# A grouped-query decode kernel on one core: the last step of V turned, output summed in PSUM, head epilogues on ScalarE

## The chip, the cores and the metric

The kernel runs on one core of a Trainium2 chip. The metric is device time in microseconds (us) of one execution; a profile's span is about 2 us shorter than the timed execution, because it runs from the first instruction to the last. Engines are named as in the profile: PE is TensorE (PEld its weight loads), DVE is VectorE, ACT is ScalarE, POOL is GpSimd, SP is SyncE, whose queue issues the large loads (SPq). "Granted clock" is the share of the full TensorE clock that the throttle let through.

## The reference, cut to what matters

One token attends over a cache of 65536 positions: 16 query heads share 8 K/V heads of width 256. K and V are 268 MB each in bf16 and are read once. The rest is small: a 448 to 4096 projection of x to q, the 4096 to 448 output projection `wo`, a one-token MLP mixer of 1792 hidden units over 448 channels, and a sigmoid gate that mixes the two.

```python
q = (x @ wq).reshape(B, Sq, Hq, Dh).transpose(0, 2, 1, 3)
scores = einsum("bhqd,bhkd->bhqk", q, repeat(k_cache, 2)) * Dh ** -0.5
p = softmax(scores);  o = einsum("bhqk,bhkd->bhqd", p, repeat(v_cache, 2))
a = o.transpose(0, 2, 1, 3).reshape(B, Sq, Hq * Dh) @ wo
b = mixer(x)          # layernorm, w1, gelu, w2
out = g * a + (1 - g) * b      # g = sigmoid(sum(x * gate_w))
```

## The kernel before

A ring of three SBUF slots of 48 KB per partition takes K and V chunks in turn: K of chunk 0, V of chunk 0, K of chunk 1 and so on. A head (`g`) has 32 steps in six chunks of 6, 6, 5, 5, 5, 5 steps. For each step DVE turns a K tile (`turn`), PE multiplies it with the queries (`scores`); after a chunk, ACT takes the exponential and PE multiplies with V (`p_v`) into four partition strips of `pv`. A slot is loaded again when the last reader of it is done: a V load waits for the last `turn` of the K that lay in its slot.

The head's epilogue runs in the first two steps of the next head (cuts are marked with `...`):

```python
def o_scale(g):                                  # DVE, after the last p_v of the head
    nc.vector.tensor_scalar(out=pvs[:], in0=pv[g % 2][:], scalar1=rden[:, 0:1], ..., op0=ALU.mult)

def o_turn(g):                                   # PE, fp32, sums the strips and turns
    ...
        nc.tensor.matmul(o_ps[:, 2*c:2*c+2], lhsT=pvs[:, lo:lo+128], rhs=sel[:, 2*half:2*half+2], ...)
    nc.vector.tensor_copy(out=oT[:], in_=o_ps)   # DVE waits for PE

def o_out(g):                                    # PE, 4 matmuls of 448 columns on one partition
    ...
        nc.tensor.matmul(a_ps, lhsT=oT[...], rhs=wo_t[g % 2][:, 2*r+c, :], ...)
    nc.vector.tensor_tensor(out=dst[:], in0=acc[:], in1=a_ps, op=ALU.add)   # DVE waits for PE

# in mixer(n), phase 5:
    nc.tensor.matmul(misc[0:1, 0:D], lhsT=w2T[:, b:b+1], rhs=gel[:], ...)
    nc.vector.scalar_tensor_tensor(out=acc[:], in0=misc[0:1, 0:D], ..., in1=acc[:], ...)  # DVE waits for PE

for i in range(total):
    for s in range(sizes[c]):
        turn(i, s, n); scores(i, s, n); mixer(n)
        if c == 0 and g > 0:
            if s == 0: o_turn(g - 1)
            if s == 1: o_out(g - 1)
    ...
```

The last chunk is loaded in pieces of one step (1 MB), in the order K0 K1 K2 K3 V0 K4 V1 V2 V3, then 10 and 6 blocks of the fifth V step. After the last piece come the last `p_v`, `o_scale`, `o_turn`, `o_out` and the output's DMA, one behind the other.

The softmax here doesn't subtract the row's maximum and nothing guards it: scores larger than these inputs give would overflow.

## Time and profile before

Three timed runs were given: 1279.43, 1280.01 and 1280.18 us.

| | before |
|---|---|
| span | 1276.4 us |
| bytes moved, mean rate | 544.9 MB, 427 GB/s |
| PE / DVE / ACT busy | 59% / 51% / 4% |
| last V piece lands | 1269.35 us |
| from there to the end | 7.05 us |

The page of before, its engine line and its DMA line (busy tenths and GB/s in 40 slices of the span):

```profile
PE 756.8 (59%) x4390; PEld 292.5 (23%) x4390; DVE 647.8 (51%) x423; ACT 51.0 (4%) x127; POOL 88.9 (7%) x147
DMA  9999999999999999999999999999999999999997
GB/s 397 434 429 431 434 438 417 429 436 434 432 418 433 431 432 436 430 430 431 431 437 424 435 432 434 435 426 432 437 433 435 421 432 433 432 437 414 434 422 309
```

No compute engine is near full, the DMA engines are busy in every slice.

```profile
SPq L97 <- DVE kT L351: 626.0, 48, 18.0
```

The end of the chain of waits of before (start, length, what):

```profile
1252.15 17.20 DMA ring_72<-in_A_v_cache_dram
...
1269.38 0.41 PE pv_76 L384 x3
...
1269.82 0.76 DVE pvs L408
...
1270.62 1.07 PE misc L417 x8
...
1271.71 0.17 DVE oT L421
...
1271.93 1.67 PE misc L427 x4
...
1273.62 0.61 DVE res L432
```

The last piece was issued at 1252.15 and landed 17.20 us later, at 1269.35; everything after is exposed.

### The profile page before, as it was taken

The numbers are of one execution on the slowest core, as the hardware profiler recorded it, in microseconds if no ns is written. First come the engines' busy times: TensorE is split into PE (matmuls) and PEld (weight loads), VectorE is DVE, ScalarE is ACT, GpSimd is POOL, SyncE is SP. The second block draws the span as 40 slices with busy tenths as digits, with TensorE's granted clock in tenths as the row PEclk, the third lists the DMA queues.
The fourth block names the chain that finished last, engine by engine and source line by source line (L and its number), as shares of the span: only waits on it lengthen the run. The fifth ranks groups of instructions, "written<-read, shape, count | busy, mean of one in ns | idle before, by whom it ended". The sixth has DMA issues, their size and how long they took to land.

```text
span 1276.4 us, 10114 instructions
## 1 busy us (share of the span) xinstructions
PE 756.8 (59%) x4390; PEld 292.5 (23%) x4390; DVE 647.8 (51%) x423; ACT 51.0 (4%) x127; POOL 88.9 (7%) x147
## 2 busy tenths in 40 slices
PE   2565567655576555765557546575565746657466
PEld 1222222221222112221222212221222312222122
DVE  4454446544465454653537345373553635536455
ACT  0000000000000000000000000000000000000000
POOL 5110202102021010210000000000000000000000
PEclk9887977878778788887779878798786977869789
DMA  9999999999999999999999999999999999999997
GB/s 397 434 429 431 434 438 417 429 436 434 432 418 433 431 432 436 430 430 431 431 437 424 435 432 434 435 426 432 437 433 435 421 432 433 432 437 414 434 422 309
DMA packets 16834, 544.88 MB, mean 427 GB/s; under 512 B 2195, under 2 KB 2326, under 8 KB 3478
## 3 DMA queue, kind: packets, MB, share of 16 engines
q1 hardware_dynamic: 15410, 540.55, 98.4%
q0 software_dynamic: 1376, 3.69, 0.8%
q8 instruction: 34, 0.56, 0.2%
q14 instruction: 10, 0.08, 0.0%
q10 hardware_dynamic: 4, 0.00, 0.0%
HBM read 544.22 MB, written 0.00 MB: 426 GB/s over the span
## 4 chain that ended last, share of the span: by engine, by line
DMA 56%; PE 23%; DVE 14%; issue 6%; ACT 1%; DVEq 0%; SPq 0%
DMA ring_70<-in_A_k_cache_dram 22%; DMA ring_71<-in_A_k_cache_dram 17%; DMA ring_72<-in_A_k_cache_dram 16%; PE sc_73 L362 16%; DVE kT_266 L354 8%; DVE kT_267 L354 4%; PE pv_75 L384 2%; PE pv_76 L384 2%; DMA ring_72<-in_A_v_cache_dram 1%; DVE pT_270 L373 1%; PE misc L417 1%; PE misc L427 1%; PE sc_74 L362 1%; ACT p_268 L369 1%; DVE acc L432 0%
## 5 line engine op out<-in xcount | busy, mean ns | idle before, releaser
L362 PEld LDWEIGHTS <-qw_283 128*128 128x128 bf16 x1024 | 110.8, 110 | 402.0 <-issue 173.8
L362 PEld LDWEIGHTS <-qw_284 128*128 128x128 bf16 x1024 | 110.1, 110 | 387.0 <-issue 155.6
L362 PE MATMUL sc_73<-kT_266,qw_284 128*128 128x512 bf16 x288 | 93.5, 480 | 108.2 <-DVE kT_266 L354 108.1
L362 PE MATMUL sc_73<-kT_266,qw_283 128*128 128x512 bf16 x288 | 92.8, 477 | 109.0 <-DVE kT_266 L354 108.7
L354 DVE STREAM_TRANSPOSE kT_266<-ring_72 128x2048 f32<-128x2048 f32 x48 | 110.1, 2294 | 73.5 <-DMA ring_72<-in_A_k_cache_dram 63.1
L354 DVE STREAM_TRANSPOSE kT_267<-ring_70 128x2048 f32<-128x2048 f32 x48 | 109.9, 2289 | 69.9 <-DMA ring_70<-in_A_k_cache_dram 61.6
L354 DVE STREAM_TRANSPOSE kT_266<-ring_71 128x2048 f32<-128x2048 f32 x40 | 91.5, 2288 | 77.6 <-DMA ring_71<-in_A_k_cache_dram 65.8
L354 DVE STREAM_TRANSPOSE kT_267<-ring_71 128x2048 f32<-128x2048 f32 x40 | 91.7, 2293 | 63.9 <-DMA ring_71<-in_A_k_cache_dram 52.0
L362 PE MATMUL sc_74<-kT_267,qw_283 128*128 128x512 bf16 x288 | 84.2, 442 | 66.1 <-DVE kT_267 L354 65.5
L354 DVE STREAM_TRANSPOSE kT_266<-ring_70 128x2048 f32<-128x2048 f32 x40 | 92.0, 2300 | 60.4 <-DMA ring_70<-in_A_k_cache_dram 43.9
L362 PE MATMUL sc_74<-kT_267,qw_284 128*128 128x512 bf16 x288 | 81.4, 430 | 61.9 <-DVE kT_267 L354 61.8
L354 DVE STREAM_TRANSPOSE kT_267<-ring_72 128x2048 f32<-128x2048 f32 x40 | 91.0, 2275 | 1.4 <-PE sc_73 L362 1.1
L362 PE MATMUL sc_74<-kT_266,qw_283 128*128 128x512 bf16 x224 | 61.6, 421 | 30.0 <-DVE kT_266 L354 30.0
L362 PE MATMUL sc_73<-kT_267,qw_284 128*128 128x512 bf16 x224 | 67.7, 453 | 16.1 <-DVE kT_267 L354 16.1
L362 PE MATMUL sc_73<-kT_267,qw_283 128*128 128x512 bf16 x224 | 65.9, 444 | 13.6 <-DVE kT_267 L354 13.6
L362 PE MATMUL sc_74<-kT_266,qw_284 128*128 128x512 bf16 x224 | 60.6, 416 | 18.3 <-DVE kT_266 L354 18.2
L373 DVE STREAM_TRANSPOSE pT_271<-p_269 128x512 bf16<-128x512 bf16 x24 | 17.1, 711 | 67.9 <-ACT p_269 L369 67.9
L373 DVE STREAM_TRANSPOSE pT_270<-p_268 128x512 bf16<-128x512 bf16 x24 | 17.1, 712 | 66.6 <-ACT p_268 L369 66.6
L369 ACT ACTIVATE p_268<-sc_73 128x512 bf16<-128x512 f32 x24 | 14.3, 597 | 652.4 <-PE sc_73 L362 652.4
L384 PEld LDWEIGHTS <-pT_270 128*4 128x4 bf16 x1024 | 22.9, 87 | 73.3 <-DVE pT_270 L373 48.9
L384 PEld LDWEIGHTS <-pT_271 128*4 128x4 bf16 x1024 | 24.1, 90 | 61.7 <-DVE pT_271 L373 32.3
L369 ACT ACTIVATE p_269<-sc_74 128x512 bf16<-128x512 f32 x24 | 14.3, 597 | 528.3 <-PE sc_74 L362 528.3
(108 smaller groups left out, 355.6 us busy)
## 6 DMA issues: line engine op xcount, KB each, us to landing
ring_71<-in_A_k_cache_dram SPq DMA_DIRECT2D x15, 5120.0 KB, 25.4
ring_72<-in_A_v_cache_dram SPq DMA_DIRECT2D x15, 5120.0 KB, 23.4
ring_70<-in_A_k_cache_dram SPq DMA_DIRECT2D x8, 6144.0 KB, 30.9
ring_71<-in_A_v_cache_dram SPq DMA_DIRECT2D x8, 6144.0 KB, 28.2
ring_72<-in_A_k_cache_dram SPq DMA_DIRECT2D x8, 6144.0 KB, 37.4
ring_70<-in_A_v_cache_dram SPq DMA_DIRECT2D x8, 6144.0 KB, 19.1
ring_70<-in_A_k_cache_dram SPq DMA_DIRECT2D x8, 5120.0 KB, 29.7
ring_71<-in_A_v_cache_dram SPq DMA_DIRECT2D x8, 5120.0 KB, 23.0
```

The source lines that it names most:

```text
L354: nc.vector.transpose(out=kT[n % 2][:].bitcast(FP32), in_=kn[:, s * SB * 128:(s + 1) * SB * 128])
L362: nc.tensor.matmul(sc[i % 2][:], lhsT=qw[g % 2][:, q, PAD - s:PAD - s + 128], rhs=kv[:, :, q // 2, :, q % 2], start=(s == 0 and q == 0), s ...
L369: nc.scalar.activation(out=p_t[i % 2][:], in_=sc[i % 2][:], func=ACT.Exp, scale=scale, accum_out=den[g % 2][:, c:c + 1],)
L373: nc.vector.transpose(out=pT_t[i % 2][:], in_=p_t[i % 2][:])
L384: nc.tensor.matmul(pv[g % 2][32 * a:32 * a + 4, :], lhsT=pT[:, k, :, s], rhs=vt[:, j * DH:(j + 2) * DH], start=first and k < 4, stop=last ...
L417: nc.tensor.matmul(o_ps[:, 2 * c:2 * c + 2], lhsT=pvs[:, lo:lo + 128], rhs=sel[:, 2 * half:2 * half + 2], start=(half == 0), stop=(half == 1),
L427: nc.tensor.matmul(a_ps, lhsT=oT[:, 2 * c + r:2 * c + r + 1], rhs=wo_t[g % 2][:, 2 * r + c, :], start=(c == 0 and r == 0), stop=(c == 1 an ...
```

## The change

The intent: shorten what follows the last byte, and take the head epilogues off DVE. Four parts:

- **New tail.** The last step of V is multiplied the other way round, V as the weights and p as two moving columns, so that its product falls straight into the turned `o_ps`. The copy and the fp32 turn cover the earlier steps only.
- **Order of the last loads.** All K pieces before all V pieces; the last piece has 4 blocks.
- **Output summed in PSUM.** Mixer and heads accumulate in one bank `acc`, 448 columns as 4 x 112 on four column strips; no DVE add.
- **Epilogues on ACT.** Copy of `pv` and scaling of `oT` are ACT instructions; the softmax denominator is applied to `oT`.

```diff
-            for s in range(last - 1):
-                piece(item - 1, s * SB, SB)
-            piece(item, 0, SB)
-            piece(item - 1, (last - 1) * SB, SB)
-            for s in range(1, last - 1):
+            for s in range(last):
+                piece(item - 1, s * SB, SB)
+            for s in range(last - 1):
                 piece(item, s * SB, SB)
-            tail = SB // 2 - 2
-            piece(item, (last - 1) * SB, SB - tail)
-            piece(item, last * SB - tail, tail)
+            piece(item, (last - 1) * SB, SB - TAIL)
+            piece(item, last * SB - TAIL, TAIL)
...
+    def to_acc(col, rows, stop=False):
+        for a in range(4):
+            nc.tensor.matmul(
+                acc[32 * a:32 * a + 1, 0:DQ], lhsT=col, rhs=rows[:, DQ * a:DQ * (a + 1)],
+                start=a not in opened, stop=stop, tile_position=(0, 32 * a),
+            )
+            opened.add(a)
...
         if ph == 5:
-            nc.tensor.matmul(misc[0:1, 0:D], lhsT=w2T[:, b:b + 1], rhs=gel[:], ...)
-            nc.vector.scalar_tensor_tensor(out=acc[:], in0=misc[0:1, 0:D], ...)
+            to_acc(w2T[:, b:b + 1], gel[:])
...
+    def p_v_turned(i, s, lo, hi):
+        for j in range(lo, hi):
+            for c in range(2):
+                at = (s * SB + j) * DH + c * 128
+                nc.tensor.matmul(
+                    o_ps[:, 2 * c:2 * c + 2], lhsT=vt[:, at:at + 128], rhs=pT[:, j, :, s],
+                    start=False, stop=(j == SB - 1 and c == 1), skip_group_check=True,
+                )
...
                 if s == 0:
                     o_turn(g - 1)
+                    for r in range(2):
+                        nc.scalar.activation(
+                            out=oT[:, r:4:2], in_=o_ps[:, r:4:2], func=ACT.Copy, scale=rden[:, r:r + 1])
...
-            o_scale(g)
+            nc.scalar.activation(out=pvs[:], in_=pv[g % 2][:], func=ACT.Copy)
...
+    nc.vector.tensor_copy(out=pvs[:, 0:DH], in_=pv[g % 2][:, 0:DH])
+    nc.scalar.activation(out=pvs[:, DH:2 * DH], in_=pv[g % 2][:, DH:2 * DH], func=ACT.Copy)
+    o_turn(g)
+    p_v_turned(i, s, 0, SB - TAIL)
+    p_v_turned(i, s, SB - TAIL, SB)
+    nc.vector.tensor_tensor(out=oT[...], in0=o_ps[...], in1=rden[...], op=ALU.mult)
+    o_out(g)
+    nc.vector.tensor_scalar(out=res[0:97, :], in0=acc[0:97, 0:DQ], scalar1=bias[0:97, 0:1], ...)
```

More of the change, by code (lines that the diff above doesn't have):

```diff
@@ L27 @@
 WIN = 128 + PAD
+TAIL = 4
 GELU_C0 = 0.7978845608028654
@@ L57 @@
     DR = D - DA
-    assert DR == 64 and F % 128 == 0 and SK % (128 * SB * sum(SIZES)) == 0
+    DQ = D // 4
+    assert DR == 64 and D % 4 == 0 and F % 128 == 0 and SK % (128 * SB * sum(SIZES)) == 0
     sizes = SIZES * (SK // (128 * SB * sum(SIZES)))
@@ L78 @@
     misc = psum.tile([128, 512], FP32, name="misc")
+    den_ps = psum.tile([128, 512], FP32, name="den_ps")
+    acc = psum.tile([128, 512], FP32, name="acc")
     total = HKV * n_chunks
@@ L132 @@
     nc.gpsimd.dma_start(out=w2T[:], in_=B_w2[:, 0].rearrange("(p b) -> p b", b=NF))
-    b2 = const.tile([1, 1], FP32)
-    nc.gpsimd.dma_start(out=b2[:], in_=B_b2.rearrange("(o n) -> o n", o=1))
+    zb = const.tile([1, 2], FP32)
+    nc.gpsimd.dma_start(out=zb[:, 1:2], in_=B_b2.rearrange("(o n) -> o n", o=1))
     wo_t = [const.tile([128, 4, D], BF16, name=f"wo{i}") for i in range(2)]
@@ L153 @@
     pick = const.tile([128, 2, len(classes)], FP32)
-    same = const.tile([128, len(classes), 64, 2], FP32)
     nc.gpsimd.memset(sel[:], 0.0)
@@ L168 @@
         nc.gpsimd.memset(block[32 * a:32 * a + 32, a:a + 1], 1.0)
-    for k in range(len(classes)):
-        nc.gpsimd.tensor_copy(
-            out=same[:, k],
-            in_=pick[:, :, k].rearrange("p (o r) -> p o r", o=1).to_broadcast([128, 64, 2]),
-        )
     mhalf = const.tile([128, 1], FP32)
@@ L189 @@
     dsum = work.tile([128, len(classes)], FP32, name="dsum")
-    rden = work.tile([128, 1], FP32, name="rden")
+    rden = work.tile([128, 2], FP32, name="rden")
     pvs = work.tile([128, 512], FP32, name="pvs")
     oT = work.tile([128, 4], BF16, name="oT")
-    acc = work.tile([1, D], FP32, name="acc")
-    half_g = work.tile([1, 1], FP32, name="half_g")
-    res = work.tile([1, D], BF16, name="res")
+    half_g = work.tile([128, 1], FP32, name="half_g")
+    bias = work.tile([128, 1], FP32, name="bias")
+    res = work.tile([128, DQ], BF16, name="res")
     qT = const.tile([128, 2, HQ], BF16)
@@ L202 @@
         nc.vector.memset(t[:], 0.0)
-    nc.vector.memset(acc[:], 0.0)
+    nc.vector.memset(acc[:, 0:DQ], 0.0)
     xd = const.tile([1, 2, 128], BF16)
@@ L226 @@
     nc.vector.tensor_tensor(out=xg, in0=x_row[:], in1=gw_row[:], op=ALU.mult)
-    z1 = const.tile([1, 1], FP32)
-    nc.vector.tensor_reduce(out=z1[:], in_=xg, axis=AXIS.X, op=ALU.add)
-    z_ps = misc[:, 500:501]
-    nc.tensor.matmul(z_ps, lhsT=one_f[:], rhs=z1[:], start=True, stop=True)
-    nc.scalar.activation(out=gate[:, 0:1], in_=z_ps, func=ACT.Exp, scale=-1.0)
-    nc.scalar.activation(out=gate[:, 1:2], in_=z_ps, func=ACT.Exp, scale=1.0)
+    nc.vector.tensor_reduce(out=zb[:, 0:1], in_=xg, axis=AXIS.X, op=ALU.add)
+    z_ps = misc[:, 500:502]
+    nc.tensor.matmul(z_ps, lhsT=one_f[:], rhs=zb[:], start=True, stop=True)
+    nc.scalar.activation(out=gate[:, 0:1], in_=z_ps[:, 0:1], func=ACT.Exp, scale=-1.0)
+    nc.scalar.activation(out=gate[:, 1:2], in_=z_ps[:, 0:1], func=ACT.Exp, scale=1.0)
     nc.vector.tensor_scalar(out=gate[:], in0=gate[:], scalar1=1.0, scalar2=None, op0=ALU.add)
     nc.vector.reciprocal(out=gate[:], in_=gate[:])
+    nc.vector.tensor_scalar(
+        out=half_g[:], in0=gate[:, 1:2], scalar1=0.5, scalar2=None, op0=ALU.mult
+    )
+    nc.vector.tensor_tensor(out=bias[:], in0=z_ps[:, 1:2], in1=gate[:, 1:2], op=ALU.mult)
     xb_ps = sc[0][:, 0:D]
@@ L307 @@
     MIX = min(8, (n_steps - 4) // (NF + 1))
+    opened = set()
+    def to_acc(col, rows, stop=False):
[5 more added lines that the diff above has]
+            opened.add(a)
     def mixer(n):
@@ L328, in mixer @@
             nc.gpsimd.tensor_scalar(
-                out=t_b[:], in0=t_b[:], scalar1=1.0, scalar2=None, op0=ALU.add
+                out=t_b[:], in0=t_b[:], scalar1=1.0, scalar2=half_g[:, 0:1], op0=ALU.add,
+                op1=ALU.mult,
             )
@@ L332, in mixer @@
         if ph == 5:
-            nc.tensor.matmul(
-                misc[0:1, 0:D], lhsT=w2T[:, b:b + 1], rhs=gel[:], start=True, stop=True
-            )
-            if b == 0:
-                nc.vector.tensor_scalar(
-                    out=half_g[:], in0=gate[0:1, 1:2], scalar1=0.5, scalar2=None, op0=ALU.mult
-                )
-                nc.vector.tensor_scalar(
-                    out=acc[:], in0=acc[:], scalar1=b2[0:1, 0:1], scalar2=gate[0:1, 1:2],
-                    op0=ALU.add, op1=ALU.mult,
-                )
-            nc.vector.scalar_tensor_tensor(
-                out=acc[:], in0=misc[0:1, 0:D], scalar=half_g[0:1, 0:1], in1=acc[:],
-                op0=ALU.mult, op1=ALU.add,
-            )
+            to_acc(w2T[:, b:b + 1], gel[:])
     def turn(i, s, n):
@@ L373, in softmax, with p_v @@
         nc.vector.transpose(out=pT_t[i % 2][:], in_=p_t[i % 2][:])
-    def p_v(i, s, lo=0, hi=SB // 2):
+    def p_v(i, s):
         g, c = divmod(i, n_chunks)
@@ L379, in p_v @@
         first = c == 0 and s == 0
-        last = c == n_chunks - 1 and s == sizes[c] - 1
-        for k in range(lo, hi):
+        last = (g, c, s) == (HKV - 1, n_chunks - 1, sizes[c] - 2)
+        last |= g < HKV - 1 and c == n_chunks - 1 and s == sizes[c] - 1
+        for k in range(SB // 2):
             j = s * SB + 2 * k
@@ L397, in den_tot @@
     def den_tot(g):
-        d_ps = misc[:, 501:502]
         for k in range(len(classes)):
             nc.tensor.matmul(
-                d_ps, lhsT=same[:, k].rearrange("p o r -> p (o r)"), rhs=dsum[:, k:k + 1],
+                den_ps[:, 0:2], lhsT=dsum[:, k:k + 1].to_broadcast([128, 128]), rhs=pick[:, :, k],
                 start=(k == 0), stop=(k == len(classes) - 1),
             )
-        nc.vector.reciprocal(out=rden[:], in_=d_ps)
-        nc.vector.tensor_tensor(out=rden[:], in0=rden[:], in1=gate[:, 0:1], op=ALU.mult)
-    def o_scale(g):
+        nc.vector.reciprocal(out=rden[:], in_=den_ps[:, 0:2])
         nc.vector.tensor_scalar(
-            out=pvs[:], in0=pv[g % 2][:], scalar1=rden[:, 0:1], scalar2=None, op0=ALU.mult
+            out=rden[:], in0=rden[:], scalar1=gate[:, 0:1], scalar2=None, op0=ALU.mult
         )
+    o_ps = misc[:, 504:508]
     def o_turn(g):
-        o_ps = misc[:, 504:508]
-        for c in range(2):
-            for half in range(2):
+        for half in range(2):
+            for c in range(2):
                 lo = half * DH + c * 128
@@ L418, in o_turn @@
                     o_ps[:, 2 * c:2 * c + 2], lhsT=pvs[:, lo:lo + 128], rhs=sel[:, 2 * half:2 * half + 2],
-                    start=(half == 0), stop=(half == 1),
+                    start=(half == 0 and c == 0), stop=(half == 1 and c == 1), skip_group_check=True,
                 )
-        nc.vector.tensor_copy(out=oT[:], in_=o_ps)
+    def p_v_turned(i, s, lo, hi):
+        vt = ring[(2 * i + 1) % RING]
+        pT = pT_t[i % 2][:].rearrange("p (j r x) -> p j r x", r=2, x=16)
+        for j in range(lo, hi):
+            for c in range(2):
+                at = (s * SB + j) * DH + c * 128
+                nc.tensor.matmul(
+                    o_ps[:, 2 * c:2 * c + 2], lhsT=vt[:, at:at + 128], rhs=pT[:, j, :, s],
+                    start=False, stop=(j == SB - 1 and c == 1), skip_group_check=True,
+                )
     def o_out(g):
-        a_ps = misc[0:1, 0:D]
         for c in range(2):
             for r in range(2):
-                nc.tensor.matmul(
-                    a_ps, lhsT=oT[:, 2 * c + r:2 * c + r + 1], rhs=wo_t[g % 2][:, 2 * r + c, :],
-                    start=(c == 0 and r == 0), stop=(c == 1 and r == 1),
-                )
-        dst = res if g == HKV - 1 else acc
-        nc.vector.tensor_tensor(out=dst[:], in0=acc[:], in1=a_ps, op=ALU.add)
+                to_acc(
+                    oT[:, 2 * c + r:2 * c + r + 1], wo_t[g % 2][:, 2 * r + c, :],
+                    stop=(g == HKV - 1 and c == 1 and r == 1),
+                )
         if g + 2 < HKV:
@@ L445 @@
                     o_turn(g - 1)
+                    for r in range(2):
+                        nc.scalar.activation(
+                            out=oT[:, r:4:2], in_=o_ps[:, r:4:2], func=ACT.Copy, scale=rden[:, r:r + 1]
+                        )
                 if s == 1:
@@ L454 @@
             den_tot(g)
-        for s in range(sizes[c]):
-            if i == total - 1 and s == sizes[c] - 1:
-                p_v(i, s, 0, SB // 4 + 1)
-                p_v(i, s, SB // 4 + 1)
-            else:
-                p_v(i, s)
+        for s in range(sizes[c] - (i == total - 1)):
+            p_v(i, s)
         if 2 * i + 1 + RING < 2 * total:
             load(2 * i + 1 + RING)
-        if c == n_chunks - 1:
-            o_scale(g)
-            if g + 1 < HKV:
-                queries(g + 1)
-    o_turn(HKV - 1)
-    o_out(HKV - 1)
-    nc.sync.dma_start(out=out[0, 0].rearrange("(o n) -> o n", o=1), in_=res[:])
+        if c == n_chunks - 1 and g + 1 < HKV:
+            nc.scalar.activation(out=pvs[:], in_=pv[g % 2][:], func=ACT.Copy)
+            queries(g + 1)
+    g, i, s = HKV - 1, total - 1, sizes[-1] - 1
+    nc.vector.tensor_copy(out=pvs[:, 0:DH], in_=pv[g % 2][:, 0:DH])
[3 more added lines that the diff above has]
+    p_v_turned(i, s, SB - TAIL, SB)
+    nc.vector.tensor_tensor(
+        out=oT[:].rearrange("p (c r) -> p c r", r=2), in0=o_ps.rearrange("p (c r) -> p c r", r=2),
+        in1=rden[:].rearrange("p (o r) -> p o r", o=1).to_broadcast([128, 2, 2]), op=ALU.mult,
+    )
+    o_out(g)
+    nc.vector.tensor_scalar(
+        out=res[0:97, :], in0=acc[0:97, 0:DQ], scalar1=bias[0:97, 0:1], scalar2=None, op0=ALU.add
+    )
+    nc.sync.dma_start(
+        out=out[0, 0].rearrange("(a n) -> a n", a=4), in_=res[0:97:32, :]
+    )
 _INS = ['A_x', 'A_k_cache', 'A_v_cache', 'A_wq', 'A_wo', 'B_x', 'B_w1', 'B_b1', 'B_w2', 'B_b2', 'gate_w']
```

## The prediction

> What bounds the kernel now. The page's slice table shows the 16 DMA engines busy in tenth 9 of all 40 slices but the last (7), and 544.9 MB moved at 427 GB/s over the 1276.4 us span. PE is busy 59%, DVE 51%, ACT 4%. Where the DMA engines' load is read in stretches of 4 us, it dips to about 0.9 (380 to 400 GB/s) once every 12 us, at the joint of two loads, and never to a stall: each load of a ring slot is issued 20 to 37 us before it lands (table of DMA issues) and takes only about 12 us of that, so one load or more is always queued. Faster compute in the body therefore buys nothing. Only what follows the last byte is exposed.
>
> That tail, in the timeline and the chain of waits of before: the last V piece lands at 1269.34; 3 matmuls of P V to 1269.79; DVE scales pv into pvs 0.75; fp32 turning matmuls 1.05; DVE cast oT 0.16; four 448-column Wo matmuls 1.65; DVE add on one partition 0.61; output DMA issued at 1274.26, span ends at 1276.4. In all 7.06 us.
>
> What the change does to it. The last step of V (16 blocks) is multiplied in turned form, V as weights, straight into o_ps, so the pvs copy and the fp32 turn cover earlier steps only. It moves them before the last landing, if they finish in time.
> - V's fourth step lands about 1.5 us before the 12-block piece does now, near 1267.0; its 8 matmuls end near 1267.8 (a step now takes 0.8 with its latency). The pvs copy is split between DVE and ACT, but ACT's copy waits for DVE's (seen in the order of the built kernels; both read one PSUM bank). The Trainium skill, "PSUM — Partial Sum Buffer", section "PSUM bank collisions raise a hardware error", asks for such guarding; no trace here shows a collision. Estimate 0.45 + 0.40, from 0.75 and 0.60 for 512 columns: 1268.75. The second half of the turn (half of 1.05) ends near 1269.3.
> - 32 turned matmuls: the q projection's 128x128 weight load and 1-column matmul pairs repeat every 26.5 ns in the start's timeline. So 24 end near 1269.95 and the last 8 near 1270.3. The fp32 turn, not the landing, is the limit by about 0.6.
> - oT multiply 0.2; 16 Wo matmuls of 112 columns on four column strips, estimate 0.7 with latency, against 1.65; add over 97 partitions x 112 columns 0.25 against 0.61; output DMA 2.1 as now.
> End near 1273.7, against 1276.4: 2.7 us less. The Wo matmuls ran at a granted clock of 0.50 (windows of the tail), which agrees with the Trainium skill, "TensorE: Matmul & The Clock Gate", Part 1 (idle halves the clock). If PE stays warm, the estimate holds; if not, add 0.4.
>
> Body: group epilogues go from DVE to ACT (0.75 per head), the mixer's 0.67 us DVE add disappears, each mixer and Wo matmul becomes four. All off the critical path: worth 0. K before V in the last loads moves the same bytes and the final softmax 2 us earlier: also 0.
>
> Prediction: 1277.4 us (0.2% faster), 1276.0 to 1279.0. Faster by over 2%: 0.01; within 2%: 0.98; slower: 0.01.
>
> Signs: DMA share and rate unchanged; last V landing within 1 us of 1269.3; from it to the end of the span 4 to 5 us; DVE busy down by about 20 us with no effect; the last turned matmuls waiting for the turn rather than for DMA.
>
> What would make it wrong: the DMA's rate drifting by 0.1% (1.3 us, half the effect); four output descriptors of 224 bytes taking longer than one of 896; turned matmuls slower than 26.5 ns; a new wait in the body starving the queue.

## More of the kernel before

The rate in the slices dips every fifth slice or so (417, 418, 424, 426, 421, 414): a head is about 157 us, five slices, and the dips are head starts.

The same trace in stretches of 2 us (columns: the stretch, its length, busy time and instructions of PE, PEld, DVE, ACT, POOL, then granted clock, DMA share, GB/s):

```profile
210.00:212.00 2.00, 2.00 (x10) 0.89 (x9) 1.45 (x2) 0.00 (x0) 0.00 (x0) 0.95 1.00 429
212.00:214.00 2.00, 1.34 (x7) 0.53 (x6) 1.25 (x1) 0.00 (x0) 0.00 (x0) 1.00 0.51 213
372.00:374.00 2.00, 0.48 (x6) 0.11 (x8) 0.92 (x2) 1.15 (x3) 0.41 (x1) 1.00 0.63 263
526.00:528.00 2.00, 1.34 (x7) 0.55 (x6) 1.40 (x1) 0.00 (x0) 0.00 (x0) 1.00 0.67 283
998.00:1000.00 2.00, 0.48 (x9) 0.15 (x12) 0.71 (x1) 0.69 (x2) 0.00 (x0) 1.00 0.81 312
1152.00:1154.00 2.00, 1.71 (x9) 0.68 (x7) 1.56 (x1) 0.00 (x0) 0.00 (x0) 1.00 0.63 270
```

At five of the seven head starts the DMA engines had too little queued for a part of 2 us. I call a head start starved if a stretch of 2 us there, counted from even microseconds, stays under 325 GB/s. The count depends on where the stretches begin; the table under e12 has it with moved stretches too. (Single stretches of 307 to 328 GB/s also occur elsewhere, at the joints of loads and where the small last loads begin.)

What delays the load there, in the timeline of before (start, length, engine, line, operation; in brackets the idle time before it and what ended it):

```profile
192.67 0.16 DVE L421 CAST oT<-misc 128x4 bf16<-128x4 f32 x1 [5.19 <-PE misc L417]
199.17 0.67 DVE L345 SCALAR_TENSOR_TENSOR acc<-misc,half_g,acc 1x448 f32<-1x448 f32 x1 [4.12 <-PE misc L333]
201.59 0.61 DVE L432 TENSOR_TENSOR acc<-acc,misc 1x448 f32<-1x448 f32 x1 [1.74 <-PE misc L427]
213.27 0.33 SPq L90 DMA_DIRECT2D ring_70<-in_A_v_cache_dram  x1
```

Each of the three DVE instructions waits for PE, and the next turn of K stands behind it in DVE's order. PE's product in turn stands behind the scores of the step before, which waited for the turn before. For two steps DVE and PE work in lock-step and not side by side, and the V load, which waits for the last turn of the chunk, goes out at 213.27. PE ran at half clock through most of this, which stretches the lock-step: eight matmuls of `scores` took 3.57 us at 195.10 and 1.90 us at 213.30.

The load queue's waits for a turn of K (the waiting line, what it waits for, total us, times, longest us), before and then after:

```profile
SPq L90 <- DVE kT_267 L354: 412.7, 24, 28.1
```

## The result, and the profile after

The changed kernel took 1273.95 us (median of 4 runs, 1273.73 to 1274.30), the kernel before 1279.72 (median of 4, 1277.56 to 1280.18). A ratio here is always the mean time of one kernel's runs over that of the other's of the same rounds, so it is not quite the ratio of the medians: 0.9958, with a 95% interval of 0.9941 to 0.9976. The class "within 2%" was right; the time lies 2 us below the low end of the predicted range of 1276.0 to 1279.0. The gain is about twice what was predicted.

| | before | after |
|---|---|---|
| span of the profile | 1276.4 | 1272.2 |
| last V piece lands | 1269.35 | 1267.64 |
| from there to the end | 7.05 | 4.56 |
| DVE busy | 647.8 | 626.8 |
| longest wait of the load queue for a turn of K | 28.1 | 18.0 |
| starved head starts | 5 | 0 |

The last landing of the changed kernel is off its chain; it is read from the trace's completion records, of which every load of 128 partitions has 16; I read them as one from each of the 16 DMA engines. So in this pair of profiles 2.5 of 4.2 us come from the tail and 1.7 from a landing that comes earlier, which the prediction had not foreseen. (Later profiles of the kernel before have this landing at 1268.29 and, in e14, at 1269.92: one pair gives no size.)

The end of the chain of waits of after:

```profile
1245.05 20.16 DMA ring<-in_A_v_cache_dram
...
1265.25 0.84 PE pv L382 x8
...
1266.11 0.44 DVE pvs L472
...
1266.59 1.05 PE misc L414 x8
1267.64 0.84 PE misc L425 x32
...
1268.51 0.17 DVE oT L477
...
1268.73 0.40 PE acc L314 x16
...
1269.15 0.33 DVE res L482
```

The chain no longer starts at the last piece but at the one before the fifth step (landed 1265.21): the turn, not the last landing, is the limit, as predicted. The 32 turned matmuls took 0.84 us, 26 ns each.

The head start in after, a stretch and two lines of the timeline, against the lines of before that are shown above:

```profile
202.00:204.00 2.00, 1.71 (x9) 0.68 (x7) 1.56 (x1) 0.00 (x0) 0.00 (x0) 1.00 1.01 429
193.04 0.42 ACT L451 ACTIVATE oT<-misc,rden 128x2 bf16<-128x2 f32 x2 [12.32 <-PE misc L414]
203.59 0.33 SPq L97 DMA_DIRECT2D ring<-in_A_v_cache_dram  x1
```

ACT takes PE's result, DVE goes on turning K, and the same V load goes out at 203.59, almost 10 us earlier. No head start starves.

One more difference, in stretches of 4 us at the end. First before:

```profile
1260.00:1264.00 4.00, 2.26 (x10) 0.76 (x8) 1.94 (x1) 0.07 (x1) 0.00 (x0) 1.00 1.01 426
1264.00:1268.00 4.00, 2.44 (x36) 1.31 (x37) 1.14 (x5) 0.62 (x2) 0.00 (x0) 1.00 0.89 369
```

Then after:

```profile
1260.00:1264.00 4.00, 2.44 (x25) 1.13 (x28) 1.21 (x5) 0.69 (x2) 0.00 (x0) 0.79 0.59 249
1264.00:1268.00 4.00, 3.20 (x47) 1.70 (x40) 0.42 (x1) 0.38 (x1) 0.00 (x0) 0.79 0.23 92
```

In after, part of the DMA engines are done long before the others. The completion records show it, without naming the engine: for the last piece the first engine is done at 1259.40 and the last at 1267.64, with seven engines inside the first 1.9 us and nine 4.8 us or more behind. In before all 16 finish between 1267.18 and 1269.34. At a starved head start the engines that are behind catch up (the spread within a load falls from 3.1 to 2.3 us over the one at 526, for instance); without starving, the spread grows to 8 us over the run. The last landing is that of the slowest engine.

### The profile page after: what moved, and what is told of

The parts are those of the page before. It is cut to its first block, busy times and chain, and to the rows that moved or that the text cites. A ratio compares the mean times of both kernels' runs of the same rounds, so it can differ in the third digit from the quotient of the medians.

```text
span 1272.2 us, 10454 instructions
## 1 busy us (share of the span) xinstructions
PE 723.6 (57%) x4552; PEld 285.1 (22%) x4552; DVE 626.8 (49%) x388; ACT 58.4 (5%) x149; POOL 78.5 (6%) x145
## 3 DMA queue, kind: packets, MB, share of 16 engines
HBM read 544.22 MB, written 0.00 MB: 428 GB/s over the span
## 4 chain that ended last, share of the span: by engine, by line
DMA 63%; PE 17%; DVE 11%; issue 8%; ACT 1%; POOL 0%; DVEq 0%; ACTq 0%; SPq 0%; POOLq 0%
DMA ring<-in_A_k_cache_dram 59%; PE sc L359 12%; DVE kT L351 9%; PE pv L382 5%; DMA zb<-in_B_b_dram 2%; DMA ring<-in_A_v_cache_dram 2%; DVE pT L370 1%; ACT p L366 1%; PE den_ps L398 0%; PE misc L270 0%; DVEq L351 0%; PE acc L314 0%; PE misc L414 0%; PE misc L274 0%; PE misc L425 0%
## 5 line engine op out<-in xcount | busy, mean ns | idle before, releaser
L359 PE MATMUL sc<-kT,qw 128*128 128x512 bf16 x2048 | 575.7, 434 | 443.8 <-DVE kT L351 442.8
L351 DVE STREAM_TRANSPOSE kT<-ring 128x2048 f32<-128x2048 f32 x256 | 575.3, 2288 | 478.1 <-DMA ring<-in_A_k_cache_dram 396.1
L359 PEld LDWEIGHTS <-qw 128*128 128x128 bf16 x2048 | 215.5, 108 | 791.5 <-DVE kT L351 332.2
L382 PE MATMUL pv<-ring,pT 128*4 128x512 bf16 x2040 | 125.7, 395 | 62.1 <-DVE pT L370 61.8
L370 DVE STREAM_TRANSPOSE pT<-p 128x512 bf16<-128x512 bf16 x48 | 34.2, 712 | 130.9 <-ACT p L366 130.9
L382 PEld LDWEIGHTS <-pT 128*4 128x4 bf16 x2040 | 46.6, 89 | 135.0 <-DVE pT L370 81.7
L366 ACT ACTIVATE p<-sc 128x512 bf16<-128x512 f32 x48 | 28.7, 597 | 1037.6 <-PE sc L359 1037.6
L336 POOL TENSOR_TENSOR t_b<-t_b,u_b 128x448 f32<-128x448 f32 x14 | 16.0, 1142 | 1.2
L343 POOL TENSOR_TENSOR gel<-t_b,u_b 128x448 bf16<-128x448 f32 x14 | 15.9, 1133 | 1.2
L414 PEld LDWEIGHTS misc<-sel,pvs 128*128 128x128 f32 x64 | 11.8, 258 | 3.7 <-issue 2.0
```

The lines of the kernel that those rows point to most:

```text
L336: nc.gpsimd.tensor_tensor(out=t_b[:], in0=t_b[:], in1=u_b[:], op=ALU.mult)
L343: nc.gpsimd.tensor_tensor(out=gel[:], in0=t_b[:], in1=u_b[:], op=ALU.mult)
L351: nc.vector.transpose(out=kT[n % 2][:].bitcast(FP32), in_=kn[:, s * SB * 128:(s + 1) * SB * 128])
L359: nc.tensor.matmul(sc[i % 2][:], lhsT=qw[g % 2][:, q, PAD - s:PAD - s + 128], rhs=kv[:, :, q // 2, :, q % 2], start=(s == 0 and q == 0), s ...
L366: nc.scalar.activation(out=p_t[i % 2][:], in_=sc[i % 2][:], func=ACT.Exp, scale=scale, accum_out=den[g % 2][:, c:c + 1],)
L370: nc.vector.transpose(out=pT_t[i % 2][:], in_=p_t[i % 2][:])
```

## The experiments

Theory: the body was not free. At head starts, the lock-step of DVE and PE delays a V load so far that the queue runs dry, and the change removes that (the body's part); the rest is the tail. Rivals: the tail is everything and the earlier landing is an accident of one profile; or DVE's work, not its waits, is what starved the queue; or the order of the loads.

### e1: the kernel before, with its DVE waits placed behind the next turn

```diff
-        nc.vector.tensor_copy(out=oT[:], in_=o_ps)
+        pend.append(cast)          # likewise the mixer's add and a head's add (which gets a bank of its own)
...
             turn(i, s, n)
+            while pend:
+                pend.pop(0)()
```

> Kernel before, with its DVE work and its old tail kept, but each DVE instruction that waits for PE (the cast of oT, the mixer's add, the add of a head's output) placed behind the next turn of K in DVE's order. Theory (lock-step of DVE and PE starves the DMA queue at head starts): no 2 us stretch under 300 GB/s between 10 and 1260 us, the longest wait of the load queue for a turn of K falls from 28 us to under 22, and the time falls by 1.5 to 4 us against the kernel before, to 1276 to 1278. Rival (the body is worth nothing, all of the gain is tail and drift): same as the kernel before, within 0.7 us, stalls as before or no effect of them.

Measured: 1276.72 us (1275.72 to 1278.56), before 1278.20, ratio 0.9989 (0.9965 to 1.0013). No head start starved; the longest wait of the load queue fell to 19.6 us, the last landing is at 1267.61. The waits of its load queue for a turn of K:

```profile
SPq L92 <- DVE kT L358: 625.1, 47, 19.6
```

The mechanism of the stalls is confirmed: same work, same engine, another place in DVE's order, and the stalls at head starts are gone. The interval of the time includes 1, because the runs of before scatter by 5 us, so the size stays open here. e3 (below), which has the whole new body with the old tail, had the ratio 0.9988: moving the waits alone did as much as the new body, as far as this can tell.

### e2 and e5: the changed kernel with the waits put back

DVE gets copies of one to a few columns that wait for PE where the old cast and adds stood.

```diff
+    def wait_pe(col, x):
+        nc.tensor.matmul(junk[0:1, 0:1], lhsT=col, rhs=x, start=True, stop=True)
+        nc.vector.tensor_copy(out=probe[0:1, 0:1], in_=junk[0:1, 0:1])
...
+            wait_pe(w2T[:, b:b + 1], gel[:, 0:1])                       # after the mixer's product
+                    nc.vector.tensor_copy(out=probe[:], in_=o_ps)       # after o_turn
+                    wait_pe(oT[:, 3:4], wo_t[(g - 1) % 2][:, 3, 0:1])   # after o_out; in e5: w2T[:, 0:1]
```

> Changed kernel with tiny DVE copies (about 0.1 us each) that wait for PE at the places where the kernel before had its cast and adds, nothing else. Theory: the waits alone bring the starved stretches at head starts back (several of 200 to 315 GB/s over 2 us) and 1.5 to 4 us of time, to 1275.5 to 1278. Rival (DVE's work, not its waits): within 0.5 us of the changed kernel.

Measured: 1361.82 us (1361.33 to 1362.32), ratio 1.0651. This was a mistake of mine, not the effect I was after: the third probe read a `wo` tile that had just been handed to its next load, and DVE waited for that load. It is instructive all the same. The load queue waited 41.8 us at the longest, and a head start looks like this (stretches of the run e2):

```profile
212.00:214.00 2.00, 0.00 (x0) 0.00 (x0) 0.00 (x0) 0.00 (x0) 0.00 (x0) 0.50 0.57 235
214.00:226.00 12.00, 7.60 (x24) 2.93 (x25) 8.25 (x5) 0.00 (x0) 0.00 (x0) 0.61 0.01 4
```

The DMA engines stood still for 12 us. This happened at six heads: 87.9 us more than the changed kernel are 14.6 us at each, for a wait that is 13.7 us longer than the 28.1 of before. At these heads the V load went out 10.7 to 11.7 us after the last DMA engine was done with the load ahead of it, so nothing was left to move; in before it went out 1.9 to 5.1 us ahead of that moment. Once the queue is empty, the wait is paid in full.

> As the earlier run with the waits put back, mended: there the third probe read a Wo tile that had just been given to its next load, and DVE waited 16 us for that load at each head. Here it reads a tile that is never loaded again. Theory: starved stretches (200 to 320 GB/s over 2 us) at most of the five head starts where the kernel before had them, time 1 to 3 us over the changed kernel, 1275 to 1277. Rival (waits of DVE for PE cost nothing): within 0.5 us of 1273.9, no starved stretch.

Measured with the mended probe: 1274.11 us (1273.87 to 1274.49), ratio 0.9968. The longest wait rose to 25.3 us, only one head start (319 GB/s at 1150) is starved (three with moved stretches), and the last landing stayed at 1267.39. My expectation failed. The waits alone bring 7 of the 10 us of delay back, and that cost no time. A reading that fits, but was not tested apart: the faster DMA engines ran dry for a moment (the spread within a load fell by 1.1 to 1.4 us at three heads), the slowest did not; the V loads went out 4.9 to 7.0 us before the slowest engine was done with the load ahead.

### e4: the changed kernel with DVE's work put back, without waits

```diff
+            nc.vector.tensor_scalar(out=dump[0:1, 0:D], in0=dump[0:1, 0:D], scalar1=1.0, ...)   # x2 per mixer block
+                    nc.vector.tensor_scalar(out=dump[:], in0=dump[:], scalar1=1.0, ...)          # x2 after o_turn
+                    nc.vector.tensor_scalar(out=dump[0:1, 0:D], ...)                             # x2 after o_out
```

> Changed kernel with DVE work added at the places of the old cast and adds, about as long as the old instructions, on SBUF alone and without a wait for PE. Theory: no starved stretch, within 0.5 us of the changed kernel. Rival (DVE's work is what starves the queue): starved stretches at head starts and 1.5 us or more.

Measured: 1273.46 us (1273.37 to 1274.04), DVE busy 646.9 us as in before, no starved head start. DVE's busy time by itself is not what costs: as the whole cause, this rival is out. Since the waits alone (e5) cost nothing measurable either, and both together do (e9 and e16), the work may still add to the delay of the V load.

### e3 and e7: the changed kernel with parts of the old tail

e3 puts back the whole tail (order of loads, last step straight, one DVE copy of `pvs` after it); e7 keeps the new order and puts back the straight last step only.

```diff
-        for s in range(sizes[c] - (i == total - 1)):
-            p_v(i, s)
+        for s in range(sizes[c]):
+            p_v(i, s)              # the last step in two parts, as in before
...
-    nc.vector.tensor_copy(out=pvs[:, 0:DH], in_=pv[g % 2][:, 0:DH])
-    nc.scalar.activation(out=pvs[:, DH:2 * DH], ...)
+    nc.vector.tensor_copy(out=pvs[:], in_=pv[g % 2][:])
     o_turn(g)
-    p_v_turned(i, s, 0, SB - TAIL)
-    p_v_turned(i, s, SB - TAIL, SB)
```

> Changed kernel with the load order and last step of before: V's last step straight, pvs copied and turned after the last landing. Theory: the turned last step is worth about 2 us of the 5.8: 1275.5 to 1277, body without starved stretches. Rival (the turned step is worth nothing, body or drift is all): 1274, within 0.5.

> Changed kernel with the new load order but V's last step straight, as before: pvs copied (0.70) and turned (1.05) after the last landing. Theory: last landing near 1267.6 as in the changed kernel, the tail behind it 1.2 to 1.8 us longer, 1275.1 to 1275.8. Rival (the turned step alone is the whole tail gain of 3 us): 1277.

Measured: e3 1277.16 us (1275.39 to 1278.23), e7 1276.42 us (1275.11 to 1276.64). Both confirm a tail worth 2.5 to 3.2 us against the changed kernel (it was not timed again); both medians are above what was expected, e3 barely, e7 by 0.6 us. The chain of waits of e7 says why:

```profile
1250.19 17.18 DMA ring<-in_A_v_cache_dram
...
1267.41 0.62 PE pv L382 x3
...
1268.05 0.70 DVE pvs L476
...
1268.80 1.88 PE misc L414 x8
```

The fp32 turn took 1.88 us in place of 1.07, at a granted clock of 0.50. The Trainium skill, "TensorE: Matmul & The Clock Gate", Part 1, says that idle PE falls to half its clock and that the window that decides is free-running. The traces agree on the two clocks: at the ends of the runs the same eight passes took 1.05 to 1.07 us where the granted clock was 1.00 and about 1.87 where it was 0.50, with both in two executions of one kernel (before and e12). No run here tests the window. An old tail of this kind has a length that depends on the execution.

### e6: the changed kernel with only the old order of loads

```diff
-            for s in range(last):
+            for s in range(last - 1):
                 piece(item - 1, s * SB, SB)
+            piece(item, 0, SB)
+            piece(item - 1, (last - 1) * SB, SB)
-            for s in range(last - 1):
+            for s in range(1, last - 1):
```

> Changed kernel with only the order of the last loads put back (the last K piece behind V's first piece). Theory (without stalls the 16 DMA engines drift apart by 7 to 8 us, so a K piece that is queued later lands much later on the slowest engine, and the last softmax with four steps of P V comes behind it): last turn of K later, the chain runs through K's last piece, 1.5 to 2.5 us slower than the changed kernel, 1275.5 to 1276.5. Rival (the order is worth nothing, as predicted): within 0.5 us of 1273.9.

Measured: 1274.16, 1274.23, 1276.42 and 1276.97 us, median 1275.32. Two runs equal the changed kernel, two are 2.3 us or more longer. The order is not worth a fixed amount: the last softmax comes later (its exponential starts at 1262.30, in the changed kernel at 1260.19), and the four steps of P V behind it then have no slack. In the profiled execution, a fast one, these 32 matmuls took 1.86 us. In the profile of after, 24 of them took 2.73 us at a granted clock near 0.52, so an estimate for 32 at such a clock is 3.6 us; with 0.8 us more for the fp32 turn this makes 2.6 us. That it is the clock which parts the two pairs of runs is therefore likely, but not shown, since only one of the four was profiled.

### e8: more PE instructions

```diff
             scores(i, s, n)
+            if i < total - 1:
+                for _ in range(8):
+                    nc.tensor.matmul(junk[0:1, 0:1], lhsT=w2T[:, 0:1], rhs=w2T[:, 0:1], ...)
```

> Changed kernel with 16 idle PE instructions (8 one-column matmuls into an unused bank) behind every step of scores: about 4000 more, 0.2 us of PE a step, PE not the limit. Theory (PE's instructions are fetched by the same DMA engines in packets of 16 KB and about 1 us each, on some engines only, which is why the engines drift apart): instruction packets 35 to about 51, ramp-down of the DMA rate at the end longer by about 3 us, time 1 to 2.5 us more. Rival (the drift has another cause): same ramp-down, within 0.5 us of 1273.9.

Measured: 1276.67 us (1276.56 to 1276.99). First the line of instruction packets of the changed kernel, then of e8 (queue: packets, MB, share of 16 engines):

```profile
q8 instruction: 35, 0.57, 0.2%
```

```profile
q8 instruction: 51, 0.84, 0.2%
```

The 16 packets of 16 KB came as expected, the last landing moved from 1267.64 to 1270.15, and the time rose by 2.7 us, a little more than expected. The ramp-down did not get longer: the spread within the last load is 8.5 us against 8.2. So idle PE instructions cost time in this kernel, which DMA bounds, and their fetch is the only DMA traffic that was added; but that the fetch explains why seven engines run ahead is not shown. It stays open.

### e9: the old body whole, with the new tail

Sums in SBUF by DVE, cast and copy on DVE, four products of 448 columns in one bank; `acc_sb` enters the accumulating bank by four small matmuls at the start of the second chunk of the last head.

```diff
+            nc.tensor.matmul(misc[0:1, 0:D], lhsT=w2T[:, b:b + 1], rhs=gel[:], start=True, stop=True)
+            nc.vector.scalar_tensor_tensor(out=acc_sb[:], in0=misc[0:1, 0:D], scalar=1.0, in1=acc_sb[:], ...)
-            to_acc(w2T[:, b:b + 1], gel[:])
...                                     (o_turn's cast, o_out's add and the pvs copy on DVE likewise)
+        if i == total - n_chunks + 1:
+            to_acc(one_f[0:1, 0:1], acc_sb[:])
```

> Changed kernel with the old body put back whole (mixer's product and a head's output summed in SBUF by DVE, cast and pvs copy on DVE, the four products of a head over 448 columns in one bank) and the new tail kept; the sum enters the accumulating bank by four small matmuls long before the end. The probes alone moved the V load at head starts from 18 to 25 us of waiting and starved only the faster DMA engines. Theory (waits and work together pass the slack of the queue): starved stretches at the head starts as in the kernel before, longest wait of the load queue near 28 us, ramp-down of the DMA rate at the end short, 1275.3 to 1276.8. Rival (the tail is the whole gain): 1273.5 to 1274.3.

Measured: 1274.46 us (1274.36 to 1276.05), ratio 0.9970. Two starved head starts (996 and 1150), longest wait 26.2 us, last landing 1267.65. The median is below what the theory expected and just above the rival's range, the highest run well above it. Inconclusive by itself: with the old body it depends on the execution how far a head start starves (with moved stretches, five of them do here). In this profile PE's clock was up at the first head start (the fp32 turn took 0.95 us, in before 1.70), and the V load went out at 211.16 and not 213.27.

### e11: one V piece on nine DMA engines

If seven engines finish 5 to 8 us early, they could take a larger share of the last loads.

```diff
+            piece(item, (last - 2) * SB, SB, ((0, 63), (63, 126), (126, 128)))   # partitions of three DMAs
```

> Changed kernel with one V piece of the last chunk (the fourth step, 1 MB) loaded by three DMAs over 63, 63 and 2 partitions. The Trainium skill (DMA: Bandwidth & Descriptors, Why a DMA increments its semaphore by 16 and not by 1) says that a DMA runs on the lowest-numbered k engines, k the largest divisor up to 16: here nine, and two. In the changed kernel's trace seven of the 16 engines finish the last piece 5 to 8 us before the last one. If the lowest-numbered nine contain the seven that are ahead: last landing 1 to 2.4 us earlier, 1271.7 to 1273. If they are the nine that are behind: 1.5 to 2.5 us later, 1275.3 to 1276.5. If such a DMA runs on all 16 after all: no change.

Measured: 1280.77 us (1280.52 to 1281.86), 6.8 us more than the changed kernel. The piece landed on the chain at 1270.62, 5.4 us later than in the changed kernel. The time moved in the direction that was expected if the nine are the ones behind, but the completion records speak against that case. Each of the two large DMAs has nine of them, as the expectation says; in the first, six came at 1257.23 to 1259.55 and three at 1266.03 to 1268.49, so the nine were six engines that are ahead and three that are behind. The load before the divided piece, itself undivided, also ended late (1266.49, against 1262.77 in the changed kernel). The size is more than twice what was expected, and the trace does not tell why (the rate from 1256 on is low throughout). It is no way to balance the engines.

### e12: the kernel before once more

> The kernel before, unchanged: a second profile and more timed runs. If the stalls of its body cost the slowest DMA engine 1.7 us, its last landing is again near 1269.3 us and it has four or more starved stretches; if that was one execution's accident, the last landing is near 1267.6. Times 1276.3 to 1282, a spread of 3 us or more, no difference from the kernel before.

Measured: 1278.87 us (1277.30 to 1279.70), ratio 0.9995. The second profile of the same kernel has the same span, 1276.4 us, made up differently: one starved head start on the grid of even microseconds (320 GB/s at 1150), five with moved stretches, longest wait 26.3 us, last landing 1268.29, but a tail of 8.1 us at half clock, against 7.05. From the end of its chain:

```profile
1233.83 24.73 DMA ring<-in_A_k_cache_dram
...
1265.11 3.83 PE pv L384 x40
...
1269.78 1.88 PE misc L417 x8
...
1271.90 1.67 PE misc L427 x4
```

Here the chain runs through the last piece of K, the last softmax and all 40 matmuls of P V, and not through the last landing: what e6 shows for the order of the loads happens in the kernel before too.

Neither of the two outcomes came out: the landing lies between them. The completion records of the profiles give a relation. "Lead" is the time from the issue of the V load at a head start to the moment when the last DMA engine is done with the load ahead of it. "Moved" counts head starts where some stretch of 2 us, moved in steps of 0.25 us around that issue, stays under 325 GB/s:

| kernel | starved head starts | moved | longest wait | lead, seven heads | last landing |
|---|---|---|---|---|---|
| before | 5 | 5 | 28.1 | 1.9 to 5.1 | 1269.34 |
| e14 (below) | 5 | 5 | 28.1 | 1.8 to 5.4 | 1269.92 |
| e12 = before | 1 | 5 | 26.3 | 3.1 to 5.9 | 1268.29 |
| e16 = e9 | 1 | 4 | 26.6 | 3.1 to 5.6 | 1268.67 |
| e9 | 2 | 5 | 26.2 | 3.6 to 6.2 | 1267.65 |
| e5 | 1 | 3 | 25.3 | 4.9 to 7.0 | 1267.39 |
| new body (after, e3, e4, e6, e7, e13, e15, e17) and e1 | 0 | 0 | 17.6 to 19.6 | 10.7 to 15.8 | 1267.30 to 1267.96 |

The old body costs the last landing 0 to 2 us, depending on the execution. The count does not order the kernels, and the wait gives no sharp threshold: in before the lowest rate (172 GB/s from 1155 to 1157) followed a wait of 25.7 us, while a head with 25.5 us stayed at 341 GB/s. The shortest lead divides them better: the landing is late (1268.29 to 1269.92) where it is 3.1 us or less, and not (1267.96 at most) where it is 3.6 us or more. With so few profiles this is a relation and not a rule.

### e13: two steps of V turned

```diff
-        for s in range(sizes[c] - (i == total - 1)):
+        for s in range(sizes[c] - 2 * (i == total - 1)):
...
+    p_v_turned(i, s - 1, 0, SB)
     p_v_turned(i, s, 0, SB - TAIL)
```

> Changed kernel with the last two steps of V turned in place of one, so that the copy and the fp32 turn come before V's fourth step has landed. Estimate from the trace of the changed kernel: the turn ends about 1266.5 in place of 1267.64, the turned matmuls of the fourth step take 0.84, and the last 8 matmuls wait for the last landing at 1267.64: 0.2 to 0.5 us less, 1273.4 to 1273.8. Rival (32 more weight loads of 128 columns cost more than they save): 1274 or more.

Measured: 1273.92 us (1273.36 to 1275.63), ratio 0.9959: no better than the changed kernel (0.9958) and more scattered. In the profiled run, its slowest, the fp32 turn fell on a granted clock of 0.50 and took 1.87 us; the 64 turned matmuls took 1.72 us, 27 ns each, as fast as at full clock.

### e14: the old tail kept warm

```diff
+    def warm(times):                       # idle matmuls of 512 columns into an unused bank
+        for _ in range(times):
+            nc.tensor.matmul(junk[:], lhsT=ident[:], rhs=kT[0][:, 0:512], start=True, stop=True)
...   # warm(8) behind the last softmax, warm(2) behind each of the last steps of p_v, warm(3) behind the last
```

> Kernel before with idle full-width matmuls put into PE's waiting times of the tail only (8 behind the last scores, 2 behind each of the last steps of P V, 3 behind the last), body and order untouched. Theory (the old tail is slow and scattered because PE often runs it at half clock): granted clock 1.0 through the tail, fp32 turn 1.05 and not 1.9, median 1 to 2 us below the kernel before, spread of its runs smaller. Rival (clock in the tail is not what costs): within 0.5 us of the kernel before, same spread.

Measured: 1279.02 us (1276.92 to 1280.51), ratio 0.9997. The clock was 1.00 through the tail and the turn took 1.07 us, as intended, yet the time did not move. It settles nothing: the profiled execution starved at all five head starts (last landing 1269.92), and PE, which takes its instructions in order, ran the fillers between the steps of P V, so that the last of those ended at 1271.62, 1.70 us after the landing, against 0.44 us in before.

### e15 to e17: the two by two table

> The changed kernel, as a corner of the table: 1273.5 to 1274.3, ratio to before 0.995 to 0.997.

> Old body, new tail (the same kernel as e9). If the tail is worth 3 to 4.5 us and the body 1 to 2: 1274.3 to 1276, ratio 0.996 to 0.998, some runs a us or more above the others where stalls at head starts fell together. If the body is worth nothing: equal to the changed kernel within 0.3 us.

> New body, old tail (the same kernel as e3). If the two add: 1276.5 to 1277.8, ratio 0.998 to 0.999, its runs scattered over 2 to 3 us by the clock of PE in the tail. If the body is worth nothing: equal to the kernel before, 1278.5 to 1279.5.

Kernels are those of after, e9 and e3, timed in the same rounds on one chip. Median, range, and ratio to before:

| | old tail | new tail |
|---|---|---|
| old body | before: 1278.27 (1276.55 to 1283.73) | e16: 1275.47 (1274.64 to 1277.67), 0.9975 (0.9957 to 0.9994) |
| new body | e17: 1276.01 (1275.02 to 1276.72), 0.9977 (0.9960 to 0.9993) | e15: 1273.64 (1273.20 to 1274.03), 0.9958 (0.9942 to 0.9975) |

With a mean of 1278.94 us for the 11 runs of before, the ratios give means of 1275.7, 1276.0 and 1273.6. The tail is worth 3.2 us with the old body and 2.4 with the new; the body is worth 2.9 us with the old tail and 2.1 with the new. The runs of e15 overlap neither those of e16 nor those of e17, so both parts are real. They nearly add: 3.2 and 2.9 make 6.1, together they save 5.3. e16 is the same kernel as e9 and took 1.0 us more than in its first call, which shows how far such a median can be trusted; likewise e17 is the same kernel as e3, whose ratio was 0.9988 and not 0.9977. From the ratios of the first calls (e3, e9 and 0.9958 for the changed kernel) the body would be worth about 1.5 us with either tail, and the tail about 3.8. What the record bears out is 1.5 to 2.9 us for the body and 2.4 to 3.8 for the tail. e17 came out 0.5 us below what was expected, the others within.

The starved head start in the profile of e16, for comparison with those of before:

```profile
1150.00:1152.00 2.00, 1.71 (x9) 0.70 (x8) 1.46 (x1) 0.00 (x0) 0.00 (x0) 1.00 0.63 270
```

## Why the prediction was wrong, point by point

- **"Faster compute in the body therefore buys nothing", "All off the critical path: worth 0."** This is the step that failed. It rested on "never to a stall", read from stretches of 4 us, of which the dips at the joints of loads hid those of the head starts; even in stretches of 4 us two head starts are at 323 and 320 GB/s (from 212 and from 1152), well under the 380 to 400 that the prediction gives, and I did not ask why. In stretches of 2 us the same trace has 213, 263, 283, 312 and 270 GB/s at five head starts. The argument "one load or more is always queued" used median times from issue to landing; at head starts, the one load that counts went out 28.1 us after its queue began to wait, only 1.9 us before the last engine was done with the load ahead of it. The new body as a whole is worth 2.1 to 2.9 us in e15 to e17. e1 shows that moving the waits in DVE's order ends the stalls; e4 shows that DVE's work alone, and e5 that the waits alone, do not cost time. How the cost divides between the waits, the work and PE's own changed products stays open.
- **The tail: "End near 1273.7, against 1276.4: 2.7 us less."** Right in mechanism and size: 2.5 us in the two profiles, 2.4 to 3.2 in the table of e15 to e17. By terms: landing to end 4.56 us, predicted 4.36; turned matmuls 26 ns, predicted 26.5; copies 0.42 and 0.38 us, predicted 0.45 and 0.40, though the second ran beside the first half of the turn; the 16 Wo matmuls 0.40, predicted 0.7; the last add 0.33, predicted 0.25; the output DMA to the end of the span 2.7, predicted 2.1. The fp32 turn was the limit, as predicted.
- **"Last V landing within 1 us of 1269.3."** Wrong: 1267.64. This is where the body's gain shows.
- **"K before V in the last loads ... worth 0."** Not so in every execution: e6 lost nothing in two runs and over 2 us in two. It may be a guard against a slow PE clock, which was argued from one profile.
- **"DVE busy down by about 20 us with no effect."** 647.8 to 626.8 us, and e4 shows that the busy time has none. The waits that went with it had.
- **ACT's copy waits for DVE's.** Seen: ACT began at 1266.57, right after DVE's copy from 1266.11. The guard that the Trainium skill asks for ("PSUM — Partial Sum Buffer") is in the built order; no run here shows a collision.
- **The range.** "The DMA's rate drifting by 0.1%" was named as the noise. The changed kernel kept within 0.6 us in its four runs; what scatters is the kernel before, by 7 us over all its runs. Its two profiles differ in the stalls and in PE's clock at the head starts and in the tail, which may be why; its slowest runs were not profiled. Three runs within 0.8 us had made it look steady.

What stays open: why seven DMA engines run ahead, how the 2.7 us of e8 come about in full, why e11's piece took so long, and how the body's gain divides. No version beat the changed kernel; e13 equals it, and e4, within noise of it, is only the changed kernel with idle work.

## What to carry to other kernels

In a kernel that is bound by DMA, the compute engines still decide when buffers come free: look at the longest wait of the load queue and at the rate in stretches well under the length of one load, not at averages, before calling compute free. Ask, too, how long before the end of the load ahead each load goes out. An instruction that waits for another engine blocks all that stands behind it on its own engine; place it behind the work that others need, or give it to an engine with nothing to do. After the last byte, leave slack for a slow PE clock: here the same old tail took 7.05 us in one execution and 8.1 in another.

## What the Trainium skill lacked or had wrong

- "DMA: Bandwidth & Descriptors", Where 436 GB/s comes from, says that for transfers between HBM and SBUF the HBM side, about 358 GB/s per core, binds. By the same page that is the share of a core when both cores of a pair stream. Here the program runs on one core, which read 544.22 MB at 428 GB/s over the whole span of the changed kernel, with stretches above 430.
- The same page does not say that the 16 DMA engines drift apart over a long run of large loads: the first and the last engine of one load were 8.2 us apart at the end of the changed kernel, in two groups of seven and nine, and 2.2 us in the kernel before, where stalls let them meet again.
- "TensorE: Matmul & The Clock Gate", LDWEIGHTS, gives a weight load as the number of columns over 1.2 GHz, 107 ns for 128, with a fast mode measured at about twice. In the trace one such load has 98 ns (mean of 32), but the loads overlap: pairs of a 128-column bf16 weight load and a matmul of two columns repeated every 26 ns at a granted clock of 1.00 and every 27 ns at 0.50 (32 in 0.84 us, 64 in 1.72 us).
- No page puts a time on the instruction stream; "Runtime: NRT & Kernel Launch", Instruction fetch mechanics, calls the cost of crossing a block of 16 KiB mostly hidden. Here 4016 more PE instructions came with 16 more packets of 16 KB, and the time rose by 2.7 us; that the fetch is the cause is not shown.
- No page puts a time on a small output in several rows: from issue to the end of the span, four rows of 224 bytes took 2.7 us and one row of 896 bytes 2.1 us (to the last landing 1.65 and 1.11 us).
